# Window attention with a gated branch, one core: the first unit's keys loaded and scored ahead of the feed-forward branch

## The chip, the cores and the metric

The kernel runs on one core of a Trainium2 chip. The metric is device time in microseconds (us); the time before is the median of three runs. Five engines work side by side, each through its own list of instructions in order: TensorE (PE, with its weight loads shown apart as PEld), VectorE (DVE), ScalarE (ACT), GpSimd (POOL) and SyncE (SP), which here does little but issue the large loads. The loads themselves are carried out by 16 DMA engines.

## The reference, cut to what matters

One decode step for two batch rows. A normalized row goes through attention over the last 4096 positions of a key and value cache (32 query heads over 8 key heads of 128), and through a small gated feed-forward branch whose result multiplies the attention's output:

```python
xn = _layernorm(x)                                   # x: (2, 1, 512)
q = (xn @ wq), 32 heads of 128
k, v = k_cache[:, :, -4096:, :], v_cache[:, :, -4096:, :]
s = softmax(q k^T / sqrt(128)) v @ wo                # wq 512 x 4096, wo 4096 x 512
z = gelu(xn @ w_in); z1, z2 = halves of z            # w_in 512 x 1792
y = (z1 * (w_sp * layernorm(z2) + b_sp)) @ w_out     # w_out 896 x 512
out = x + s * silu(y)
```

All is float32. The inputs are read once: w_q and w_o are 8192 KB each, w_in 3584 KB, w_out 1792 KB, and the keys and values in use 65536 KB together.

## The kernel before, in words

**Units.** The 2 batch rows times 8 key heads are taken in pairs: 8 units, numbered by `u.n`, each with one load of keys (`u.k`) and one of values (`u.v`), 4096 KB apiece.

**The ring.** Everything large goes through one tile, `ring`, of four slots of 4096 KB. `enqueue` puts a load into a list and gives it the next slot (w_q takes two); `advance(slot)` marks a slot as free and issues from the head of the list whatever now has its slot. All these loads are issued by SP, in the order of the list, so one that waits for its slot holds back those behind it. The order before is w_q (slots 0 and 1), w_in (2), w_out (3), keys 0 (0), keys 1 (1), values 0 (2), keys 2 (3), values 1 (0), keys 3 (1) and so on, and at the end w_o in pieces. A one-column copy of `rs`, the normalization's factor, into slot 2 stands ahead of the second load, so that this load is issued after it.

**The order on the engines.** PE, DVE, ACT and SP run what is written, in the order in which it is written (the class `InOrder`). First come the queries: `q_ps` on PE, `qT`, `qm` on DVE, `rp` on PE, `qbd` on DVE. Then the feed-forward branch: `z` on PE from w_in; a row of short steps on DVE, ACT and PE (`zs`, `zt`, `zT`, `u`, `mean`, `var`, `hT`); `y` on PE from w_out; `ys`, `yq` and `gate`. Then the units.

**A unit.** Its keys are transposed on DVE in four quarters (`turn`, tile `kt`, three buffers); each quarter is multiplied with the queries on PE (`shares`, tile `sh`), copied by ACT to `shs`, and added into `s` (`add_shares`). The maximum and the exponentials of a unit (`share_max`, tiles `m`, `mg`, `mo`, `nb`; `probs`) come in the next unit, between its first and its second quarter, and its values (`values`, tile `acc`) behind that. Keys are freed after the fourth quarter's transpose, values after `acc`.

**The end.** After the last unit, w_o is multiplied in blocks as its pieces land (`part`, `so`), and `res` is formed with `gate` and written out. `gate` is read nowhere else.

Of the kernel before, what the change touches and what calls it, by code (L numbers as in the profile page):

```python
# [9 lines left out]
F32 = mybir.dt.float32  # L10
AF = mybir.ActivationFunctionType
ALU = mybir.AluOpType
AX = mybir.AxisListType

P = 128
HQ, DH = 32, 128
G = 4
EPS = 1e-5
# [3 lines left out]
def ap(t, offset, dims):  # L22

    return bass.AP(tensor=t.tensor, offset=t.offset + offset, ap=[list(t.ap[0])] + [list(d) for d in dims])
# [18 lines left out]
def kernel(  # L43
# [14 lines left out]
    pe, dve, act, sp = (InOrder(tc, e) for e in (nc.tensor, nc.vector, nc.scalar, nc.sync))  # L58
    B, _, D = x.shape
# [4 lines left out]
    FH = F // 2  # L64
    KT = D // P
    FT = FH // P
    DC = D // G
    SCALE = DH ** -0.5
    NU = B * HKV // 2
# [7 lines left out]
    sb = ctx.enter_context(tc.tile_pool(name="sb", bufs=2))  # L77
# [7 lines left out]
    def enqueue(load, count=1):  # L85

        at = turns[0] % 4
        turns[0] += count
        queue.append((load, range(at, at + count)))
        advance()  # L90

    def advance(*slots):
        for n in slots:
            free[n] = True
        while queue and all(free[n] for n in queue[0][1]):
            load, at = queue.pop(0)
            for n in at:
                free[n] = False
            load(ring[:, at[0] * SLOT : (at[-1] + 1) * SLOT], at[0])

    def const(name, *shape):
        return cst.tile([P, *shape], F32, tag=name, name=name)

    def bank(name, tag):
        return ps.tile([P, 512], F32, tag=tag, name=name, bufs=BANKS[tag])


    weight = {}

    def load_rows(name, w, k):  # L110
        def load(t, at):
            n = k * w.shape[1]
            sp.dma_start(t[:, :n], w.rearrange("(p k) f -> p (k f)", p=P))
            weight[name] = t[:, :n].rearrange("p (k f) -> p k f", k=k)

        return load
# [8 lines left out]
    def load_unit(cache, u, name):  # L125

        first = cache[u.b, 2 * u.w, SK - W :, :]
        src = bass.AP(tensor=first.tensor, offset=first.offset, ap=[[SLOT, P // 2], [SK * DH, 2], [1, SLOT]])

        def load(t, at):  # L130
            sp.dma_start(t, src)
            setattr(u, name, t.rearrange("p (j d) -> p j d", d=DH))
            u.slot[name] = at

        return load
# [4 lines left out]
    units = []  # L140
    for n in range(NU):
        u = Unit()
# [30 lines left out]
    wb1 = cst.tile([1, 2], F32, tag="wb1", name="wb1")  # L173
    act.dma_start(wb1[:, 0:1], bass.AP(tensor=w_sp.tensor, offset=w_sp.offset, ap=[[1, 1], [1, 1]]))
    act.dma_start(wb1[:, 1:2], bass.AP(tensor=b_sp.tensor, offset=b_sp.offset, ap=[[1, 1], [1, 1]]))
    xnT = const("xnT", KT, 32)
    nc.gpsimd.memset(xnT, 0.0)
    ones = const("ones", P)
    nc.gpsimd.memset(ones, 1.0)
    hT = const("hT", FT, 32)  # L180
# [14 lines left out]
    rowm = const("rowm", 32)  # L195
# [4 lines left out]
    def rsqrt(dst, a, tag):  # L200
        t = cst.tile(list(a.shape), F32, tag="rt" + tag, name="rt" + tag)
        act.activation(t, a, AF.Ln)
        act.activation(dst, t, AF.Exp, scale=-0.5)
        dve.tensor_mul(t, dst, dst)
        dve.tensor_mul(t, t, a)
        dve.tensor_scalar(t, t, -0.5, 1.5, op0=ALU.mult, op1=ALU.add)
        dve.tensor_mul(dst, dst, t)
# [9 lines left out]
    rsqrt(rs, va, "x")  # L217

    dve.tensor_copy(ring[:B, 2 * SLOT : 2 * SLOT + 1], rs)
    enqueue(load_rows("in", w_in, KT))  # L220
    enqueue(load_rows("out", w_out, FT))
    win, wout = weight["in"], weight["out"]
    for n in range(NU + 1):
        if n < NU:
            enqueue(load_unit(k_cache, units[n], "k"))
        if n > 0:
            enqueue(load_unit(v_cache, units[n - 1], "v"))
# [41 lines left out]
    for k in range(KT):  # L269
        for r in range(2):  # L270
            for g in range(G):
                c = (r * G + g) * 512
                pe.matmul(
                    pq[r][32 * g : 32 * g + 32, :], xnT[:, k, :], wqt[:, k, c : c + 512],
                    start=(k == 0), stop=(k == KT - 1),
# [17 lines left out]

    def q_of(u, dq):
        return ap(qbd, (u.n * 4 + dq) * 32, [[1, 32]])


    FQ = FH // G
    pz = bank("z", "sh")[:, : 2 * FQ]
    for k in range(KT):  # L300
        for g in range(G):
            pe.matmul(
                pz[32 * g : 32 * g + 32, :], xnT[:, k, :], ap(win[:, k, :], g * FQ, [[FH, 2], [1, FQ]]),
                start=(k == 0), stop=(k == KT - 1),
            )
    advance(2)
    wb_ps = bank("wb_ps", "mo")[:, :2]
    pe.matmul(wb_ps, ones[0:1, :], wb1, start=True, stop=True)
    wb = const("wb", 2)
    dve.tensor_copy(wb, wb_ps)  # L310
    zs = const("zs", 2 * FQ)
    act.activation(zs, pz, AF.Copy)
    zt = const("zt", 2 * FT, 32)
    dve.transpose(zt.rearrange("p j c -> p (j c)"), ap(zs, 0, [[FQ, 2], [1, FT], [FT, 32]]))
    zT = const("zT", 2, FT, B)
    zTf = zT.rearrange("p h j b -> p (h j) b")
    dve.tensor_copy(zTf, zt[:, :, :B])
    uu = const("u", 2, FT, B)
    dve.tensor_mul(uu, zT, zT)
    dve.tensor_scalar(uu, uu, 0.044715, 1.0, op0=ALU.mult, op1=ALU.add)  # L320
    dve.tensor_mul(uu, uu, zT)
    dve.tensor_scalar(uu, uu, -2.0 * math.sqrt(2.0 / math.pi), 80.0, op0=ALU.mult, op1=ALU.min)
    act.activation(uu, uu, AF.Exp)
    dve.tensor_scalar_add(uu, uu, 1.0)
    dve.reciprocal(uu, uu)
    dve.tensor_mul(zT, zT, uu)

    z1, z2, w2 = zT[:, 0], zT[:, 1], uu[:, 0]
    mean, var = const("mean", B), const("var", B)

    def mean_over_rows(dst, src, name):
        pm = bank(name, "mo")[:, : FT * B]
        pe.matmul(pm, ones, src.rearrange("p j b -> p (j b)"), start=True, stop=True)
        dve.reduce_sum(dst, pm.rearrange("p (j b) -> p b j", b=B), axis=AX.X)

    per_b = [[0, FT], [1, B]]
    mean_over_rows(mean, z2, "mean_ps")
    dve.scalar_tensor_tensor(z2, ap(mean, 0, per_b), -1.0 / FH, z2, op0=ALU.mult, op1=ALU.add)
    dve.tensor_mul(w2, z2, z2)
    mean_over_rows(var, w2, "var_ps")  # L340
    dve.tensor_scalar(var, var, 1.0 / FH, EPS, op0=ALU.mult, op1=ALU.add)
    rsqrt(mean, var, "z")
    dve.tensor_mul(z2, z2, ap(mean, 0, per_b))
    dve.tensor_scalar(z2, z2, wb[:, 0:1], wb[:, 1:2], op0=ALU.mult, op1=ALU.add)
    dve.tensor_mul(hT[:, :, 0 : 16 * B : 16], z1, z2)


    def spread_quarters(dst, shares, start=True, stop=True):
        for g in range(G):
            pe.matmul(  # L350
                dst[32 * g : 32 * g + 32, :], rowm, shares[:, g * DC : (g + 1) * DC], start=start, stop=stop,
            )

    yp = bank("y", "sh")
    for j in range(FT):
        g = j % G
        pe.matmul(yp[32 * g : 32 * g + 32, :], hT[:, j, :], wout[:, j, :], start=(j < G), stop=(j >= FT - G))
    advance(3)
    ys = sb.tile([P, D], F32, tag="shs", name="ys")
    act.activation(ys, yp, AF.Copy)  # L360
    y = bank("yq", "mo")[:, :DC]
    spread_quarters(y, ys)
    gate = const("gate", DC)
    dve.tensor_scalar(gate, y, -1.0, 80.0, op0=ALU.mult, op1=ALU.min)
    act.activation(gate, gate, AF.Exp)
    dve.tensor_scalar_add(gate, gate, 1.0)
    dve.reciprocal(gate, gate)
    dve.tensor_mul(gate, gate, y)


    def turn(u, m):

        u.kt[m] = sb.tile([P, JC, DH], F32, tag="kt", name=f"kt{u.n}_{m}", bufs=3)
        dve.transpose(
            u.kt[m].rearrange("p j d -> p (j d)"), u.k[:, JC * m : JC * m + JC, :].rearrange("p j d -> p (j d)")
        )
# [104 lines left out]
    def collect_last(u):  # L481
# [6 lines left out]
        dve.reduce_sum(ol[r, :], t.rearrange("p (j n) -> p n j", j=NCH), axis=AX.X)  # L488
        divide(u.b, ol[r, :], r)

    prev = old = None
    last = units[-1]
    for u in units:
        turn(u, 0)
        shares(u, 0)
        if old is not None and old.n == NU // B - 1:
            divide(0, gather(0))
        if prev is not None:
            share_max(prev)
            probs(prev)  # L500
        turn(u, 1)
        shares(u, 1)
        add_shares(u, 0)
        if prev is not None:
            probs_t(prev)
            weigh(prev)
            if u is not last:
                values(prev)
        for m in range(2, NCH):
            turn(u, m)  # L510
            shares(u, m)
            add_shares(u, m - 1)
        if u is not last and prev is not None:
            scale_out(prev)
        advance(u.slot["k"])
        add_shares(u, NCH - 1)
        if u is not last and prev is not None:
            advance(prev.slot["v"])
            collect(prev)
        old, prev = prev, u  # L520
# [20 lines left out]
    for n in range(EARLY):  # L541
        t, a = blocks[n]
        g = n % G
# [4 lines left out]
    for n in range(EARLY, 32):  # L548
# [3 lines left out]
        for g in range(G):  # L552
            pe.matmul(
                so[32 * g : 32 * g + 32, :], oT[:, n, :], t[:, a, g * DC : (g + 1) * DC],
                start=(n == EARLY), stop=(n == 31),
# [33 lines left out]
```

## Time and profile before

| | |
|---|---|
| median of three runs | 217.49 us (217.29 to 217.51) |
| span of the profiled execution, first to last instruction | 215.6 us; its own time is not listed, the median is 1.9 us above the span |
| read from memory | 89.40 MB, 415 GB/s over the span |
| share of the span that the loads' queue kept the 16 DMA engines | 96.9% |
| busy: PE, DVE, ACT | 144.9, 107.1, 43.7 us |
| mean granted TensorE clock | 0.885 |

Busy times are sums over a whole span, and the engines overlap; none of them is the time by itself. Nearly all instructions stand under one source line, the helper that records the order, so rows are told apart by tile names: in `kt<-ring` the tile left of the arrow is written and that on the right is read. In the timeline a row gives the start, the duration (of a run of like instructions together where it ends in x5), and in brackets the idle time ahead of it and what ended it.

### The profile page before, as it was taken

To read this page: it belongs to the slowest core of one execution; us is meant where nothing else is said; L and a number is where in the kernel's file an instruction comes from. 1 tells how busy PE (TensorE), PEld (TensorE's weight loads), DVE (VectorE), ACT (ScalarE), POOL (GpSimd) and SP (SyncE) were. 2 spreads that over 40 slices of the span, in tenths; PEclk is the share of its full clock that TensorE was granted. 3 is DMA by queue.
4 is the path that set the end of the run, shared out by engine and by line. 5 is a ranking of instruction groups with operands and counts; after the bars stand their busy time and mean duration, and the time that the engine had idled before them with its cause. 6 is when DMAs were issued, how large, how long until landed. Compare 5 with 4: busy or idle time off the path is not lost.

```text
span 215.6 us, 2181 instructions
## 1 busy us (share of the span) xinstructions
PE 144.9 (67%) x848; PEld 40.3 (19%) x848; DVE 107.1 (50%) x161; ACT 43.7 (20%) x108; POOL 4.2 (2%) x22
## 2 busy tenths in 40 slices
PE   0010787224595897699599499459949967987663
PEld 0010222100021222122122132112202211222311
DVE  1140025633995943953936663793585089233101
ACT  2030000331124115114303304130331231241001
POOL 6010000000000000000000000000000000000000
PEclk9999999658599699699799789859975996999998
DMA  9898999999999999999999999999999999999990
GB/s 389 390 389 389 431 423 459 435 438 421 450 395 474 395 453 419 444 432 425 439 404 450 419 444 429 432 432 419 444 413 447 425 432 444 425 435 404 410 376 33
DMA packets 3788, 89.52 MB, mean 415 GB/s; under 512 B 434, under 2 KB 450, under 8 KB 964
## 3 DMA queue, kind: packets, MB, share of 16 engines
q1 hardware_dynamic: 3772, 89.40, 96.9%
q8 instruction: 6, 0.10, 0.2%
q14 instruction: 2, 0.02, 0.0%
q10 hardware_dynamic: 8, 0.00, 0.0%
HBM read 89.40 MB, written 0.00 MB: 415 GB/s over the span
## 4 chain that ended last, share of the span: by engine, by line
DMA 41%; PE 39%; DVE 16%; ACT 2%; issue 2%; DVEq 0%
DMA ring<-in_A_wo_dram 20%; PE sh L37 11%; DMA ring<-in_A_k_cache_dram 11%; DVE kt L37 10%; DMA ring<-in_A_wq_dram 10%; PE s L37 10%; PE acc L37 7%; PE q_ps L37 4%; PE y L37 2%; PE z L37 1%; PE col L37 1%; PE mo L37 1%; DVE gate L37 1%; DVE u L37 1%; DVE qm L37 1%
## 5 line engine op out<-in xcount | busy, mean ns | idle before, releaser
L37 DVE STREAM_TRANSPOSE kt<-ring 128x2048 f32<-128x2048 f32 x32 | 72.2, 2286 | 24.9 <-DMA ring<-in_A_k_cache_dram 24.9
L37 PE MATMUL sh<-kt,qbd 128*32 128x512 f32 x256 | 43.6, 725 | 27.0 <-DVE kt L37 27.0
L37 ACT ACTIVATE shs<-sh 128x512 f32<-128x512 f32 x32 | 19.1, 597 | 99.4 <-PE sh L37 99.4
L37 PE MATMUL s<-shs,add_dq 128*128 128x512 f32 x64 | 39.0, 716 | 0.0
L37 PE MATMUL acc<-ring,pT 128*32 128x512 f32 x256 | 31.3, 614 | 0.0
L37 PEld LDWEIGHTS s<-shs,add_dq 128*128 128x128 f32 x64 | 11.0, 215 | 30.9 <-issue 26.5
L37 PEld LDWEIGHTS sh<-kt,qbd 128*32 128x32 f32 x256 | 7.0, 117 | 46.3 <-issue 38.3
L37 PE MATMUL q_ps<-ring,xnT 128*32 128x512 f32 x64 | 8.8, 713 | 7.6 <-DMA ring<-in_A_wq_dram 7.6
L37 PEld LDWEIGHTS acc<-ring,pT 128*32 128x32 f32 x256 | 7.8, 112 | 22.3 <-issue 17.6
L37 DVE TENSOR_REDUCE m<-s 128x2 f32<-128x512 f32 x8 | 5.4, 680 | 13.0 <-PE s L37 12.9
L37 PE MATMUL xnT_ps<-ident,xn 2*128 2x2 f32 x4 | 0.6, 252 | 14.5 <-DVE xn L37 14.5
L37 ACT ACTIVATE o<-acc,diag 128x128 f32<-128x128 f32 x30 | 8.6, 374 | 4.9 <-PE acc L37 4.9
L37 PE MATMUL part<-ring,oT 128*32 128x512 f32 x56 | 6.6, 597 | 3.5 <-DMA ring<-in_A_wo_dram 3.5
L37 ACT ACTIVATE p<-s,nb 128x256 f32<-128x256 f32 x16 | 7.6, 488 | 6.6 <-DVE nb L37 6.4
L37 DVE STREAM_TRANSPOSE qT<-q_ps 128x512 f32<-128x512 f32 x2 | 1.4, 717 | 14.4 <-PE q_ps L37 14.3
L37 PE MATMUL col<-o,sel 128*32 128x512 f32 x14 | 7.3, 601 | 0.0
L37 DVE TENSOR_TENSOR res<-so,gate 128x128 f32<-128x128 f32 x1 | 0.3, 292 | 11.5 <-PE so L37 11.5
L37 DVE STREAM_TRANSPOSE pT<-p 128x512 f32<-128x512 f32 x8 | 5.4, 674 | 1.2 <-ACT p L37 1.2
L37 PE MATMUL y<-ring,hT 128*32 128x512 f32 x14 | 3.3, 996 | 3.8 <-DVE hT L37 3.8
L37 ACT ACTIVATE zs<-z 128x448 f32<-128x448 f32 x1 | 0.5, 544 | 24.7 <-PE z L37 24.7
L37 ACT ACT_TABLE_LOAD x4 | 5.1, 1283 | 0.8 <-PEq L575 0.7
L37 PEld LDWEIGHTS q_ps<-ring,xnT 128*32 128x32 f32 x64 | 2.5, 130 | 13.1 <-issue 13.1
(114 smaller groups left out, 62.2 us busy)
## 6 DMA issues: line engine op xcount, KB each, us to landing
ring<-in_A_k_cache_dram SPq DMA_DIRECT2D x8, 4096.0 KB, 20.0
ring<-in_A_v_cache_dram SPq DMA_DIRECT2D x8, 4096.0 KB, 28.1
ring<-in_A_wo_dram SPq DMA_DIRECT2D x1, 4096.0 KB, 33.2
ring<-in_B_w_in_dram SPq DMA_DIRECT2D x1, 3584.0 KB, 17.1
ring<-in_A_wo_dram SPq DMA_DIRECT2D x1, 2048.0 KB
ring<-in_B_w_out_dram SPq DMA_DIRECT2D x1, 1792.0 KB, 21.0
ring<-in_A_wo_dram SPq DMA_DIRECT2D x1, 1024.0 KB
ring<-in_A_wo_dram SPq DMA_DIRECT2D x4, 256.0 KB, 17.6
```

What stands on the lines that cost most here:

```text
L37: return self.tc.keep_in_program_order(call(*args, **kwargs))
```

## The change

Keys 0 are put into the list right behind w_q, and w_in and w_out behind them. The loop leaves keys 0 out. The branch becomes the function `form_gate`, called ahead of unit 1, so that all of unit 0's transposes, products and sums stand ahead of `z` on the engines. Keys 0 now have slot 2, w_in slot 3, w_out slot 0; from keys 1 on each load has the slot that it had. `advance` is called with 3 after `z` (before: 2) and with 0 after `y` (before: 3).

```diff
     dve.tensor_copy(ring[:B, 2 * SLOT : 2 * SLOT + 1], rs)
+    enqueue(load_unit(k_cache, units[0], "k"))
     enqueue(load_rows("in", w_in, KT))
     enqueue(load_rows("out", w_out, FT))
-    win, wout = weight["in"], weight["out"]
     for n in range(NU + 1):
-        if n < NU:
+        if 0 < n < NU:
             enqueue(load_unit(k_cache, units[n], "k"))
         if n > 0:
             enqueue(load_unit(v_cache, units[n - 1], "v"))
...
-    FQ = FH // G
-    pz = bank("z", "sh")[:, : 2 * FQ]
-    for k in range(KT):
...
-    advance(2)
...
-        pe.matmul(yp[32 * g : 32 * g + 32, :], hT[:, j, :], wout[:, j, :], start=(j < G), stop=(j >= FT - G))
-    advance(3)
...
+    def form_gate():
+        FQ = FH // G
+        pz = bank("z", "sh")[:, : 2 * FQ]
+        for k in range(KT):
...
+        advance(3)
...
+            pe.matmul(yp[32 * g : 32 * g + 32, :], hT[:, j, :], weight["out"][:, j, :], start=(j < G), stop=(j >= FT - G))
+        advance(0)
...
+        dve.tensor_mul(gate, gate, y)
+        return gate
+
     prev = old = None
     last = units[-1]
     for u in units:
+        if u.n == 1:
+            gate = form_gate()
         turn(u, 0)
         shares(u, 0)
```

SP's list of loads before, from its start (`in_A_wq_dram` is w_q, `in_B_w_in_dram` w_in, `in_B_w_out_dram` w_out, and the caches are keys and values by name):

```order
L37 DMA ring<-in_A_wq_dram 128x16384
L37 DMA ring<-in_B_w_in_dram 128x7168
L37 DMA ring<-in_B_w_out_dram 128x3584
L37 DMA ring<-in_A_k_cache_dram 128x1x8192 x2
L37 DMA ring<-in_A_v_cache_dram 128x1x8192
```

And after:

```order
L37 DMA ring<-in_A_wq_dram 128x16384
L37 DMA ring<-in_A_k_cache_dram 128x1x8192
L37 DMA ring<-in_B_w_in_dram 128x7168
L37 DMA ring<-in_B_w_out_dram 128x3584
L37 DMA ring<-in_A_k_cache_dram 128x1x8192
L37 DMA ring<-in_A_v_cache_dram 128x1x8192
```

Keys 0 moved ahead of both weights; the list is the same from keys 1 on.

On PE, behind the queries' `rp`, stood before the branch and then unit 0 (the last row is unit 0's first product):

```order
L37 MATMUL rp<-qm,same 128x256
L37 MATMUL z<-ring,xnT 32x448 x16
L37 MATMUL wb_ps<-wb_74,ones 128x2
L37 MATMUL mean_ps<-zT,ones 128x14
L37 MATMUL var_ps<-u,ones 128x14
L37 MATMUL y<-ring,hT 32x512 x7
L37 MATMUL yq<-ys,rowm 32x128 x4
L37 MATMUL sh_0_283<-kt_0_281,qbd 32x512 x4
```

And after, from the same place:

```order
L37 MATMUL rp<-qm,same 128x256
L37 MATMUL sh_0_203<-kt_0_201,qbd 32x512 x4
L37 MATMUL sh_1_212<-kt_1_210,qbd 32x512 x4
L37 MATMUL s_219<-shs_0_208,add_dq 128x512
L37 MATMUL sh_2_223<-kt_2_221,qbd 32x512 x4
L37 MATMUL s_219<-shs_1_217,add_dq 128x512
L37 MATMUL sh_3_233<-kt_3_231,qbd 32x512 x4
L37 MATMUL s_219<-shs_2_228,add_dq 128x512
L37 MATMUL s_219<-shs_3_238,add_dq 128x512
L37 MATMUL z<-ring,xnT 32x448 x16
```

`z` and all behind it in the branch now wait for the eight groups of unit 0; unit 1's first product, which stood behind unit 0's last sum, stands behind `yq`.

On DVE the last rows of the branch and the transposes of units 0 and 1 stood before as follows:

```order
L37 TENSOR_TENSOR gate<-gate,yq 128x128
L37 STREAM_TRANSPOSE kt_0_281<-ring 128x2048
L37 STREAM_TRANSPOSE kt_1_290<-ring 128x2048
L37 STREAM_TRANSPOSE kt_2_301<-ring 128x2048
L37 STREAM_TRANSPOSE kt_3_311<-ring 128x2048
L37 STREAM_TRANSPOSE kt_0_323<-ring 128x2048
```

And after, from the queries' last step to the branch's first two:

```order
L37 TENSOR_SCALAR qbd<-rp,grpm 128x64x4 x4
L37 STREAM_TRANSPOSE kt_0_201<-ring 128x2048
L37 STREAM_TRANSPOSE kt_1_210<-ring 128x2048
L37 STREAM_TRANSPOSE kt_2_221<-ring 128x2048
L37 STREAM_TRANSPOSE kt_3_231<-ring 128x2048
L37 COPY wb<-wb_ps 128x2
L37 STREAM_TRANSPOSE zt<-zs 128x448
```

Unit 0's four transposes moved from behind `gate` to ahead of `wb`; unit 1's first one (`kt_0_323`) now follows `gate` directly.

More of the change, by code (lines that the diff above doesn't have):

```diff
@@ L295, in q_of @@
         return ap(qbd, (u.n * 4 + dq) * 32, [[1, 32]])
-    FQ = FH // G
-    pz = bank("z", "sh")[:, : 2 * FQ]
-    for k in range(KT):
[L301 to L305, printed above, removed]
-    advance(2)
-    wb_ps = bank("wb_ps", "mo")[:, :2]
-    pe.matmul(wb_ps, ones[0:1, :], wb1, start=True, stop=True)
-    wb = const("wb", 2)
@@ L310 @@
[L310 to L345, printed above, removed]
@@ L348, in spread_quarters @@
[L348 to L356, printed above, removed]
-        pe.matmul(yp[32 * g : 32 * g + 32, :], hT[:, j, :], wout[:, j, :], start=(j < G), stop=(j >= FT - G))
-    advance(3)
-    ys = sb.tile([P, D], F32, tag="shs", name="ys")
-    act.activation(ys, yp, AF.Copy)
@@ L361 @@
[L361 to L368, printed above, removed]
     def turn(u, m):
@@ L489, in collect_last, with spread_quarters, mean_over_rows @@
         divide(u.b, ol[r, :], r)
+    def spread_quarters(dst, shares, start=True, stop=True):
+        for g in range(G):
+            pe.matmul(
+                dst[32 * g : 32 * g + 32, :], rowm, shares[:, g * DC : (g + 1) * DC], start=start, stop=stop,
+            )
+    def form_gate():
+        FQ = FH // G
+        pz = bank("z", "sh")[:, : 2 * FQ]
+        for k in range(KT):
+            for g in range(G):
+                pe.matmul(
+                    pz[32 * g : 32 * g + 32, :], xnT[:, k, :], ap(weight["in"][:, k, :], g * FQ, [[FH, 2], [1, FQ]]),
+                    start=(k == 0), stop=(k == KT - 1),
+                )
+        advance(3)
+        wb_ps = bank("wb_ps", "mo")[:, :2]
+        pe.matmul(wb_ps, ones[0:1, :], wb1, start=True, stop=True)
+        wb = const("wb", 2)
+        dve.tensor_copy(wb, wb_ps)
+        zs = const("zs", 2 * FQ)
+        act.activation(zs, pz, AF.Copy)
+        zt = const("zt", 2 * FT, 32)
+        dve.transpose(zt.rearrange("p j c -> p (j c)"), ap(zs, 0, [[FQ, 2], [1, FT], [FT, 32]]))
+        zT = const("zT", 2, FT, B)
+        zTf = zT.rearrange("p h j b -> p (h j) b")
+        dve.tensor_copy(zTf, zt[:, :, :B])
+        uu = const("u", 2, FT, B)
+        dve.tensor_mul(uu, zT, zT)
+        dve.tensor_scalar(uu, uu, 0.044715, 1.0, op0=ALU.mult, op1=ALU.add)
+        dve.tensor_mul(uu, uu, zT)
+        dve.tensor_scalar(uu, uu, -2.0 * math.sqrt(2.0 / math.pi), 80.0, op0=ALU.mult, op1=ALU.min)
+        act.activation(uu, uu, AF.Exp)
+        dve.tensor_scalar_add(uu, uu, 1.0)
+        dve.reciprocal(uu, uu)
+        dve.tensor_mul(zT, zT, uu)
+        z1, z2, w2 = zT[:, 0], zT[:, 1], uu[:, 0]
+        mean, var = const("mean", B), const("var", B)
+        def mean_over_rows(dst, src, name):
+            pm = bank(name, "mo")[:, : FT * B]
+            pe.matmul(pm, ones, src.rearrange("p j b -> p (j b)"), start=True, stop=True)
+            dve.reduce_sum(dst, pm.rearrange("p (j b) -> p b j", b=B), axis=AX.X)
+        per_b = [[0, FT], [1, B]]
+        mean_over_rows(mean, z2, "mean_ps")
+        dve.scalar_tensor_tensor(z2, ap(mean, 0, per_b), -1.0 / FH, z2, op0=ALU.mult, op1=ALU.add)
+        dve.tensor_mul(w2, z2, z2)
+        mean_over_rows(var, w2, "var_ps")
+        dve.tensor_scalar(var, var, 1.0 / FH, EPS, op0=ALU.mult, op1=ALU.add)
+        rsqrt(mean, var, "z")
+        dve.tensor_mul(z2, z2, ap(mean, 0, per_b))
+        dve.tensor_scalar(z2, z2, wb[:, 0:1], wb[:, 1:2], op0=ALU.mult, op1=ALU.add)
+        dve.tensor_mul(hT[:, :, 0 : 16 * B : 16], z1, z2)
+        yp = bank("y", "sh")
+        for j in range(FT):
+            g = j % G
+            pe.matmul(yp[32 * g : 32 * g + 32, :], hT[:, j, :], weight["out"][:, j, :], start=(j < G), stop=(j >= FT - G))
+        advance(0)
+        ys = sb.tile([P, D], F32, tag="shs", name="ys")
+        act.activation(ys, yp, AF.Copy)
+        y = bank("yq", "mo")[:, :DC]
+        spread_quarters(y, ys)
+        gate = const("gate", DC)
+        dve.tensor_scalar(gate, y, -1.0, 80.0, op0=ALU.mult, op1=ALU.min)
+        act.activation(gate, gate, AF.Exp)
+        dve.tensor_scalar_add(gate, gate, 1.0)
+        dve.reciprocal(gate, gate)
+        dve.tensor_mul(gate, gate, y)
+        return gate
```

## The prediction
> **What bounds the kernel now.** I read the page's slices first, then the windows, then the loads' issues. In the slices the second row is the busy share of the 16 DMA engines in tenths:
>
> ```profile
> DMA  9898999999999999999999999999999999999990
> GB/s 389 390 389 389 431 423 459 435 438 421 450 395 474 395 453 419 444 432 425 439 404 450 419 444 429 432 432 419 444 413 447 425 432 444 425 435 404 410 376 33
> q1 hardware_dynamic: 3772, 89.40, 96.9%
> ```
>
> The engines of the loads are busy in every slice but the last, while PE and DVE have idle slices. Two windows show how steady that is (the last two columns are the DMA share and GB/s):
>
> ```profile
> 25.00:195.00 170.00, 129.36 (x712) 34.71 (x706) 100.11 (x131) 39.34 (x100) 0.00 (x0) 0.86 1.00 431
> 2.00:212.00 210.00, 144.44 (x842) 40.19 (x843) 105.94 (x158) 42.47 (x108) 2.75 (x12) 0.89 0.99 423
> ```
>
> From 25 to 195 us the share is 1.00 at 431 GB/s. So the stream of loads is the bound: 89.4 MB at the whole stream's 423 GB/s are 211 us. What is left is a start of about a microsecond and the tail. The chain of waits seems to say something else, since over its first 130 us it runs through PE and DVE; but it ends in loads that were in a queue:
>
> ```profile
> 125.88 4.41 DVE kt L37 x2
> 130.31 22.99 DMA ring<-in_A_k_cache_dram
> 168.72 33.24 DMA ring<-in_A_wo_dram
> 211.99 0.47 PE so L37 x8
> ```
>
> A load of 4096 KB that "takes" 22.99 us at 431 GB/s (4.19 MB, 9.7 us of work) stood over 13 us behind others. The instruction that released its issue was therefore not what it waited for, and what the chain shows ahead of 130.31 is not a bound. The second sign is DVE, which from unit 3 on waits for keys; the bracket is the idle time ahead of the row:
>
> ```profile
> 95.10 2.31 DVE L37 STREAM_TRANSPOSE kt<-ring 128x2048 f32<-128x2048 f32 x1 [2.37 <-DMA ring<-in_A_k_cache_dram]
> 114.57 2.31 DVE L37 STREAM_TRANSPOSE kt<-ring 128x2048 f32<-128x2048 f32 x1 [4.89 <-DMA ring<-in_A_k_cache_dram]
> DVE kt L37 <- DMA ring<-in_A_k_cache_dram: 24.9, 5, 8.0
> ```
>
> Five units of the eight wait for their keys, 24.9 us together. Keys 3 landed at 95.10 and keys 4 at 114.57, with one load of values between: 19.47 us for two loads, 9.74 us each.
>
> **The change part by part.** *Loads.* No byte, no load and no shape is added; two small weights and one load of keys change places. If the stream never runs dry its end stays, so the term is 0. It remains to show that it doesn't run dry. SP's issues, and the first two weights' time from issue to landing (last number):
>
> ```profile
> 13.92 0.34 SPq L37 DMA_DIRECT2D ring<-in_B_w_in_dram  x1
> 28.10 3.99 SPq L37 DMA_DIRECT2D ring<-in_A_k_cache_dram  x2
> 50.60 0.54 SPq L37 DMA_DIRECT2D ring<-in_A_k_cache_dram  x1
> 62.78 0.54 SPq L37 DMA_DIRECT2D ring<-in_A_v_cache_dram  x1
> 75.84 0.54 SPq L37 DMA_DIRECT2D ring<-in_A_k_cache_dram  x1
> 92.76 0.54 SPq L37 DMA_DIRECT2D ring<-in_A_k_cache_dram  x1
> ring<-in_B_w_in_dram SPq DMA_DIRECT2D x1, 3584.0 KB, 17.1
> ring<-in_B_w_out_dram SPq DMA_DIRECT2D x1, 1792.0 KB, 21.0
> ```
>
> w_in landed at 13.92 + 17.1 = 31.0, w_out (issued right behind it) at 35.3. w_q landed when PE began the queries:
>
> ```profile
> 22.67 8.81 PE L37 MATMUL q_ps<-ring,xnT 128*32 128x512 f32 x64 [7.57 <-DMA ring<-in_A_wq_dram]
> 34.40 3.21 PE L37 MATMUL z<-ring,xnT 128*32 128x448 f32 x32
> ```
>
> So w_in takes 8.4 us and w_out 4.3. Landings in the new order: w_q 22.7, keys 0 32.4, w_in 40.8, w_out 45.1, and then as before keys 1 54.8, values 0 64.6, keys 2 74.3, values 1 84.1, keys 3 at about 94 (95.10 in the trace, so these deadlines are on the early, strict side).
>
> *Unit 0.* Its rows before, and the branch's last:
>
> ```profile
> 34.50 1.66 DVE L37 TENSOR_SCALAR qbd<-rp,grpm 128x256 f32<-128x256 f32 x4 [0.85 <-PE rp L37]
> 53.87 11.07 DVE L37 STREAM_TRANSPOSE kt<-ring 128x2048 f32<-128x2048 f32 x5
> 66.50 0.69 DVE L37 TENSOR_REDUCE m<-s 128x2 f32<-128x512 f32 x1 [1.56 <-PE s L37]
> 68.53 2.31 DVE L37 STREAM_TRANSPOSE kt<-ring 128x2048 f32<-128x2048 f32 x1
> ```
>
> Keys 0 are there at 32.4, the queries (`qbd`) are formed at 36.2, so the first transpose moves from 53.87 to 36.2. The four take 4 x 2.21 = 8.9 us (11.07 over 5) and end at 45.1. Unit 0's sums ended at 66.50, 12.6 us after the first transpose: now at 48.8.
>
> *The branch.* `z` stands on PE behind those sums: it starts at 48.8, though w_in is there at 40.8; before it started at 34.40. From `z` to the end of `gate` DVE came to 53.87, 19.5 us; that chain is serial and is taken whole: it ends at 68.3. Nobody but the last multiplication at 212 us reads `gate`, which covers its lateness. But unit 1's first transpose stands right behind it on DVE. Before it started at 53.87 + 4 x 2.21 = 62.7; now at 68.3. Of those 5.6 us the 1.56 us come back that `m` waited for the sums, which are now long done: 68.3 + 2.2 + (68.53 - 66.50) = 72.5 for unit 1's second quarter against 68.53. **Unit 1 comes 4.0 us later**, not earlier: unit 0's tail on PE lay beside unit 1's first transpose before, and now nothing lies beside the branch's short steps.
>
> *The queue, issue by issue* (each must come before the landing of the load ahead). w_out now waits for slot 0, which the first half of the queries frees at 28.10, against w_in's 40.8: 12.7 us to spare; keys 1, behind it, follow at some 31.5 as before (the second issue of the row that starts at 28.10 and lasts 3.99, less half a microsecond). Values 0 wait for unit 0's fourth transpose: 45.1 against 54.8. Keys 2 wait for `z`: 52.0 against 64.6. Values 1 wait for `y`: before, that was 50.60 - 34.40 = 16.2 us behind `z`, now 65.0 against 74.3. Keys 3 wait for unit 1's fourth transpose: 75.84 + 4.0 = 79.8 against 84.1. Keys 4: 92.76 + 4.0 = 96.8 against 104.8 (their own landing less 9.74). The narrowest is keys 3 with 4.3 us (8.3 before). From issue to first byte I allow 1.3 us, an estimate from the first slice of 5.4 us, which moved as many bytes as the three behind it though the first load was issued only at 0.73 us; 3.0 us remain. Later issues meet more slack, because units 3 and 4 wait for keys: 2.37 and then 4.89 us of idle take up 4.0, and from unit 4 on everything stands where it stood.
>
> [...] PE's clock matters to this margin; the same matmul of 512 columns took (min, median, max):
>
> ```profile
> L37 PE MATMUL y<-ring,hT x14: 754/1060/1061, 47.2 to 49.8; 128*32 128x512 f32 x14
> L37 PE MATMUL part<-ring,oT x56: 590/592/617, 202.1 to 209.9; 128*32 128x512 f32 x56
> 47.20:50.60 3.40, 3.33 (x14) 0.58 (x14) 0.00 (x0) 0.00 (x0) 0.00 (x0) 0.57 0.98 424
> 40.00:45.00 5.00, 1.19 (x4) 1.00 (x4) 1.83 (x10) 2.66 (x4) 0.00 (x0) 0.50 0.98 419
> 58.50:66.50 8.00, 7.99 (x36) 1.83 (x40) 6.44 (x3) 2.12 (x4) 0.00 (x0) 0.88 1.06 455
> ```
>
> `y` ran at a granted clock of 0.57 behind a stretch in which PE had little to do (0.50). `z` ran right behind the queries; now it comes behind unit 0's products, whose clock was 0.88. I take 3.2 us for it. At the low clock it would be 3.2 x 1060 / 592 = 5.7 us, and keys 3 would be issued at 82.3: still before 84.1, with half a microsecond left after the first byte's 1.3. [...]
>
> *The tail* is untouched:
>
> ```profile
> 211.50 0.92 PE L37 MATMUL so<-ring,oT 128*32 128x128 f32 x16
> 212.81 0.29 DVE L37 TENSOR_TENSOR res<-res,x 128x128 f32<-128x128 f32 x1
> ```
>
> *Sum:* loads 0, unit 0 and branch 0 (beside the loads), queue 0, tail 0. The span stays 215.6 us, and with the 1.9 us by which the median of the runs lies above it, 217.5.
>
> **The rivals.** *Slower: unit 1's lateness drains the queue at keys 3.* For it: the narrowest place becomes half as wide, and the branch's length in its new place is borrowed from another one. Against it: it takes 3.0 us more than the 4.0 worked out. Bounds: with `z` and unit 0's sums at full clock the lateness is some 3 us, with `z` slow 6.5. If the sums and unit 1's products were slow too (another 2 to 4 us), it would be up to 10, and the stream would stand still for up to 3.5 us, which nothing gives back, since the stream is full afterwards. It decides from an issue of keys 3 at 82.8 on; half of that price gives 217.5 + 1.7 = 219.2. Chance 0.10. *Faster: the stream itself runs better.* The first slices show 389 GB/s against 431 later. If the large load of keys behind w_q let all of it go at 431, the 211 us of stream would shrink by 1 - 423/431, 1.9 per cent or 4 us: 213.5. Against it: w_q, the same load as before, fills those four slices. Chance 0.03. [...] *Faster: the chain of waits is right after all,* and work done 17.7 us earlier shortens it. By the same chain, though, unit 1 is 4.0 us late, so it would rather give 217.5 + 4.0 = 221.5; DVE's waits for keys speak against both signs, and I leave 0.03 to the gain (at most to the floor of the stream, some 215) and 0.02 to the loss. *The change doesn't do what it says:* if keys 0's landing gave nothing to unit 0, all would stand as before, at 217.5; that lies within the forecast.
>
> **How the numbers follow.** No change has 0.82, slower 0.12 (queue 0.10, chain 0.02), faster 0.06. What a measurement can tell from no change is about 0.2 per cent, 0.43 us; the three runs spread over 0.22. The time is the likeliest case's, 217.5; its own range is 217.1 to 217.9. The range is 217.0 to 218.3: it leaves out the gains and the upper part of the loss, together less than 0.15, and takes in a stand-still of up to 0.8 us.
>
> **What the changed profile would show.** Right: the DMA row full of nines with no dip between 70 and 90 us; unit 0's first transpose near 36, `z` near 49, `gate` done near 68, keys 3 issued near 80; DVE's wait for keys 3 gone, that for keys 4 near 3.3 us instead of 4.89, and keys 4 and later at the same times as before. Wrong: keys 3 issued after 83 and less than 400 GB/s in the windows from 80 to 90; keys 4 landing other than at 114.6 by more than half a microsecond; or an end that moves while DVE's waits for keys stay.

## The result, and the profile after

The changed kernel takes 219.72 us (median of five runs, 219.15 to 219.90) against 217.29 us, the median of five runs of the kernel before. The medians are 2.43 us apart; the ratio on record, which is not the quotient of these two medians, is 1.0088 (95% interval 1.0070 to 1.0106). The change makes the kernel slower by about 1 per cent. The profiled execution took 219.9 us and has a span of 218.0, 2.4 more than before. Here and below, ratios leave out slow executions, more than 1.5 per cent above the fastest of the same kernel, while medians and ranges take in all.

The slices of the page after (DMA share in tenths, GB/s, and the queue's total):

```profile
DMA  9889999999999997989899999999999999999980
GB/s 385 386 385 403 463 420 437 400 439 466 403 463 398 463 403 289 460 385 481 385 481 383 469 397 463 403 463 403 460 403 457 406 451 415 451 415 422 411 347 17
q1 hardware_dynamic: 3772, 89.40, 96.1%
```

The sixteenth slice (81.8 to 87.2 us) has 289 GB/s where its neighbours have 403 and 460; before, no slice but the last two was below 389. SP's issues around it, from the timeline, and the window from 80 us (last two columns: DMA share, GB/s):

```profile
66.82 0.53 SPq L37 DMA_DIRECT2D ring<-in_A_v_cache_dram  x1
82.86 0.54 SPq L37 DMA_DIRECT2D ring<-in_A_k_cache_dram  x1
80.00:85.00 5.00, 5.00 (x34) 1.29 (x38) 5.00 (x3) 0.56 (x1) 0.00 (x0) 0.80 0.86 321
85.00:90.00 5.00, 5.00 (x30) 1.21 (x22) 0.02 (x1) 2.06 (x6) 0.00 (x0) 1.00 0.98 410
```

Keys 3 are issued at 82.86 instead of 75.84. The two windows lack some 1.6 us of loads against 433 GB/s ((433 - 321) x 5 / 433 = 1.3 and 0.3). What delayed the issue is seen on DVE and PE:

```profile
37.25 8.88 DVE L37 STREAM_TRANSPOSE kt<-ring 128x2048 f32<-128x2048 f32 x4
50.11 3.21 PE L37 MATMUL z<-ring,xnT 128*32 128x448 f32 x32
70.32 2.30 DVE L37 STREAM_TRANSPOSE kt<-ring 128x2048 f32<-128x2048 f32 x1
75.54 2.31 DVE L37 STREAM_TRANSPOSE kt<-ring 128x2048 f32<-128x2048 f32 x1
107.44 0.69 DVE L37 TENSOR_REDUCE m<-s 128x2 f32<-128x512 f32 x1 [5.12 <-PE s L37]
DVE kt L37 <- DMA ring<-in_A_k_cache_dram: 6.2, 2, 3.9
```

Unit 0 starts 16.6 us earlier (37.25 against 53.87), and unit 1's second transpose comes 7.0 us later (75.54 against 68.53). DVE waits for keys in two units instead of five, 6.2 us instead of 24.9: the engines now run behind the loads through most of the kernel. The end, where w_o is multiplied:

```profile
205.13 7.77 PE L37 MATMUL part<-ring,oT 128*32 128x512 f32 x56 [0.68 <-DVE oT L37]
213.93 0.80 PE L37 MATMUL so<-ring,oT 128*32 128x128 f32 x16
205.00:210.00 5.00, 4.87 (x32) 1.27 (x36) 0.07 (x1) 0.00 (x0) 0.00 (x0) 0.67 0.96 397
```

and the same stretch before:

```profile
202.09 3.64 PE L37 MATMUL part<-ring,oT 128*32 128x512 f32 x32 [1.74 <-DMA ring<-in_A_wo_dram]
206.91 1.92 PE L37 MATMUL part<-ring,oT 128*32 128x512 f32 x16 [1.17 <-DMA ring<-in_A_wo_dram]
209.41 1.07 PE L37 MATMUL part<-ring,oT 128*32 128x512 f32 x8 [0.58 <-DMA ring<-in_A_wo_dram]
```

Before, PE waited for w_o three times, 3.5 us together. After, it waits for no load there: the 56 products run in one go, with a granted clock of 0.67 in the window from 205 us. The loads end late as well, as the windows from 210 us show, before and then after (the last number is GB/s):

```profile
210.00:215.00 5.00, 2.19 (x48) 0.95 (x40) 0.58 (x2) 0.60 (x1) 0.00 (x0) 0.89 0.12 47
210.00:215.00 5.00, 4.49 (x68) 1.54 (x60) 0.20 (x1) 0.60 (x1) 0.00 (x0) 1.00 0.42 157
```

At 210 us 0.24 MB were still to come before and 0.79 MB after, about 1.3 us of loads more. So there are two candidates for the 2.4 us: the stream, which stood still, and the engines, which come late to the end.

### The profile page after: what moved, and what is told of

It is laid out like the page before. It is cut to its first block, busy times and chain, and to the rows that moved or that the text cites. A ratio compares the mean times of both kernels' runs of the same rounds, so it can differ in the third digit from the quotient of the medians.

```text
span 218.0 us, 2176 instructions
## 1 busy us (share of the span) xinstructions
PE 148.0 (68%) x848; PEld 40.9 (19%) x848; DVE 106.9 (49%) x161; ACT 43.7 (20%) x108; POOL 4.2 (2%) x22
## 4 chain that ended last, share of the span: by engine, by line
PE 65%; DVE 19%; DMA 10%; ACT 3%; issue 2%; DVEq 0%; ACTq 0%
PE s L37 18%; PE sh L37 16%; PE acc L37 13%; DVE kt L37 10%; DMA ring<-in_A_wq_dram 10%; PE q_ps L37 4%; PE part L37 4%; PE col L37 2%; PE y L37 2%; PE mo L37 2%; PE z L37 1%; DVE qbd L37 1%; DVE gate L37 1%; DVE u L37 1%; DVE mx L37 1%
## 5 line engine op out<-in xcount | busy, mean ns | idle before, releaser
L37 PE MATMUL sh<-kt,qbd 128*32 128x512 f32 x256 | 45.1, 710 | 28.3 <-DVE kt L37 28.3
L37 PE MATMUL s<-shs,add_dq 128*128 128x512 f32 x64 | 40.9, 745 | 0.0
L37 PEld LDWEIGHTS s<-shs,add_dq 128*128 128x128 f32 x64 | 11.3, 219 | 29.3 <-issue 24.9
L37 PE MATMUL q_ps<-ring,xnT 128*32 128x512 f32 x64 | 9.3, 749 | 7.5 <-DMA ring<-in_A_wq_dram 7.5
L37 PE MATMUL part<-ring,oT 128*32 128x512 f32 x56 | 7.8, 715 | 0.7 <-DVE oT L37 0.7
L37 DVE TENSOR_REDUCE mx<-mo 128x1 f32<-128x16 f32 x8 | 1.4, 174 | 8.3 <-PE mo L37 8.3
## 6 DMA issues: line engine op xcount, KB each, us to landing
ring<-in_B_w_out_dram SPq DMA_DIRECT2D x1, 1792.0 KB, 18.7
```

The lines of the kernel that those rows point to most:

```text
L37: return self.tc.keep_in_program_order(call(*args, **kwargs))
```

## The experiments

**Lateness alone.** The kernel before, with transposes ahead of unit 1 whose result is not used:

```diff
     for u in units:
+        if u.n == 1:
+            for _ in range(3):
+                dve.transpose(spare, u.k[:, :JC, :].rearrange("p j d -> p (j d)"))
         turn(u, 0)
```

> The kernel before with three further transposes on DVE (3 x 2.21 = 6.6 us, their result is not used) ahead of unit 1; loads and branch as before. Queue theory (unit 1's lateness drains the queue of loads at keys 3): keys 3 issued at 75.84 + 6.6 = 82.4, a stand-still of about 1 us near 83 us, 218.4 to 219.6. Rival order of loads (keys 0 between w_q and the weights makes the stream itself slower): the order is that of before, so 217.3. Rival engines' chain (the lateness is carried along PE and DVE to the end, not through the loads): 219 to 220 as well, but the keys of units 6 and 7 land as before.

Measured: 220.9 us, ratio 1.0153 (1.0111 to 1.0196), runs from 219.81 to 224.4. With the loads in their old order the time rises all the same, so the order of the loads is not needed for the loss. It rises by more than either theory said. The trace doesn't tell them apart: the profiled execution was the longest of the six (224.4 us), in it unit 0 itself came 3.1 us late (56.99) and unit 1 9.4 us, keys 3 were issued at 85.29, and DVE waited for unit 7's keys until 177.20 instead of 172.86.

With two transposes instead of three:

> The kernel before with two further transposes (4.4 us) ahead of unit 1, loads and branch as before. By the step on record (4 us of lateness cost nothing): 217.3 to 217.7. Theory of two ends: no stand-still where PE's clock holds up (keys 3 issued at 80.3), the chain 4.4 us late at unit 1 and some 1 to 2 at the end, 217.5 to 218.8, with a wide spread from the clock. Order of loads as a cause: 217.4.

Measured: 217.89 us, 1.0029 (1.0004 to 1.0054), eight of twelve runs at 218.1 or below and the others up to 221.2. In the profiled execution unit 1 was 3.6 us late, keys 3 were issued at 79.47, and the span was 215.6, as before. The median lies above the 217.7 that the step on record allows, and within what the theory of two ends expected. Some 4 us of lateness are free in most executions, not in all.

**Keys 3 in two halves**, the first issued ahead of unit 1's third transpose: the stand-still is taken away and unit 1 left late. `load_half` issues one half; its definition, and the second half in the list's place of keys 3, are left out here.

```diff
+        if u.n == 1:
+            units[3].slot["k"] = u.slot["k"]
+            load_half(units[3], 0)
         for m in range(2, NCH):
             turn(u, m)
```

> The changed kernel with the load of keys 3 cut in two: the first half is issued behind unit 1's second transpose (near 77.9 us), the second behind its fourth (82.9). Unit 1 stays as late as in the changed kernel. Queue theory: no stand-still, 217.2 to 217.7. Rival engines' chain: still 219.0 to 219.9, since nothing on PE, DVE or ACT comes earlier. Rival order of loads: 219.0 to 219.9.

Measured: 219.24 us, 1.0081 (1.0049 to 1.0112). The queue theory said 217.2 to 217.7 and falls as the only cause. Its window and its end:

```profile
80.00:85.00 5.00, 5.00 (x38) 1.16 (x40) 4.46 (x3) 0.00 (x1) 0.00 (x0) 0.84 0.92 393
74.99 2.30 DVE L37 STREAM_TRANSPOSE kt<-ring 128x2048 f32<-128x2048 f32 x1
204.67 7.78 PE L37 MATMUL part<-ring,oT 128*32 128x512 f32 x56 [0.68 <-DVE oT L37]
213.48 0.62 PE L37 MATMUL so<-ring,oT 128*32 128x128 f32 x16
210.00:215.00 5.00, 3.75 (x64) 1.53 (x56) 0.58 (x2) 0.60 (x1) 0.00 (x0) 1.00 0.16 60
```

The loads hardly stop any more (393 GB/s instead of 321), and at 210 us 0.30 MB were left, nearly as little as before. Unit 1 is 6.5 us late, and PE still runs the last 56 products in one go, without a wait for w_o. Here the engines' chain alone sets the end.

**Two ends.** So the time is the later of two: the last landing of w_o with what follows it, and the engines' chain with its 56 products. The next three kernels put two short matmuls ahead of these products, so that PE has less idle time there.

```diff
     t = gather(last.b)
+    w2 = bank("warm_end", "sh")
+    pe.matmul(w2, ones, qT[:, :512], start=True, stop=True)
...
     collect_last(last)
+    pe.matmul(w2[:, :256], ones, qT[:, :256], start=True, stop=True)
```

With keys 3 in halves:

> The kernel with keys 3 in two halves (no stand-still of the stream, unit 1 as late as in the changed kernel) plus two further matmuls on PE, 512 columns behind the last oT product and 256 behind ol, so that PE has less idle time ahead of the last w_o products; their result is not used. Theory of two ends (the time is set by the later of the stream's last landing and the engines' chain, whose last stretch ran at half clock for 3.4 us): the 56 part matmuls take 6.6 instead of 7.8 us, 217.8 to 218.4, against 219.24 without the two matmuls. Queue theory alone (the engines' chain doesn't set the end): 219.2, no change. If the stream's last landing sets it in that kernel: 219.2, no change.

Measured: 218.40 us, 1.0032 (1.0012 to 1.0053). In the changed kernel, with its stand-still:

> The changed kernel with the two further matmuls ahead of the last w_o products and nothing else. Theory of two ends: its stream lands 1.7 to 2.3 us late by the stand-still, so the faster part matmuls gain little, 218.9 to 219.6 (against 218.4 where the stand-still was away as well). If only the engines' chain sets the end: about 218.6, as much gained as with keys 3 in halves.

Measured: 218.93 us, 1.0054 (1.0034 to 1.0074). In the kernel before, as a control:

> Control: the kernel before with the same two matmuls ahead of the last w_o products. The stream's last landing sets the end there, so both theories say 217.3 to 217.7; a gain of more than half a microsecond would mean that PE's last stretch sets the end before, too.

Measured: 217.54 us, 0.9991 (0.9973 to 1.0009). The rows of the first two, in this order (the execution of the second is the longest of its eight, 219.83 us):

```profile
205.51 6.21 PE L37 MATMUL part<-ring,oT 128*32 128x512 f32 x56
```

```profile
206.13 5.36 PE L37 MATMUL part<-ring,oT 128*32 128x512 f32 x48
211.88 1.07 PE L37 MATMUL part<-ring,oT 128*32 128x512 f32 x8 [0.39 <-DMA ring<-in_A_wo_dram]
```

With keys 3 in halves the 56 products take 6.2 instead of 7.8 us, at a granted clock of 1.00 instead of 0.71 in the window from 205 us, and the time falls by 0.8 us. With the stand-still left in, PE waits for w_o again (0.39): the stream's end has taken over in that trace. The kernel before gains nothing. Away with the stand-still or with the slow products alone, most of the loss stays. The times by themselves don't separate the two ends, though: the two matmuls gained 0.8 us with the stand-still left in, too (219.72 to 218.93). That there are two ends rests on the waits for w_o in the traces.

**PE's clock in the branch.** Four groups of three further matmuls in PE's idle stretches between 34 and 70 us (three of the calls are left out here):

```diff
+    def keep_busy(n):
+        w = bank("warm", "acc")
+        for i in range(n):
+            pe.matmul(w, ones, qT[:, :512], start=True, stop=True)
...
         dve.tensor_copy(wb, wb_ps)
+        keep_busy(3)
```

> The changed kernel with four groups of three further matmuls of 512 columns on PE (their result is not used), in its idle stretches: ahead of unit 0, behind the wb, var and yq products. If the half clock of PE in the branch's stretch is what made unit 1 3 us later than the 4.0 worked out: y 3.6 to 2.0 us, unit 1's first product 1.9 to 1.1, keys 3 issued at 80.5 to 81.5 and a time of 217.3 to 218.3. If the clock has no part in it: keys 3 at 82.9, 219.0 to 219.9, or later where the further matmuls stand in the way.

Measured: 217.57 us, 1.0005 (0.9987 to 1.0024); ten of twelve runs lie between 217.40 and 217.93, two at 218.81 and 219.09. The loss is gone in the median though order and loads are those of the changed kernel. The profiled execution is the one at 218.81. In it `y` took half as long as in the changed kernel (3.63 us), but the 56 products at the end still took 7.9 us and waited for no load:

```profile
63.80 1.92 PE L37 MATMUL y<-ring,hT 128*32 128x512 f32 x14 [1.58 <-DVE hT L37]
204.26 7.89 PE L37 MATMUL part<-ring,oT 128*32 128x512 f32 x56 [0.68 <-DVE oT L37]
```

With the two matmuls at the end as well:

> The kernel whose PE is kept busy through the branch (217.57) plus the same two matmuls ahead of the last w_o products. Theory of two ends: unit 1 is 4.7 us late, the chain ends within a microsecond of the stream, and the runs near 219 (part at half clock) go away: median 217.4 to 217.7, highest below 218.3. If the spread has another cause: runs near 219 remain.

Measured: 217.52 us, 0.9993 (0.9981 to 1.0006), highest 217.83. The window from 58 to 82 us of the changed kernel and then of this one, with this one's second transpose of unit 1 and its issue of keys 3:

```profile
58.00:82.00 24.00, 11.44 (x48) 2.88 (x52) 13.43 (x24) 4.81 (x11) 0.00 (x0) 0.50 1.00 430
58.00:82.00 24.00, 18.73 (x90) 5.08 (x93) 16.22 (x24) 4.82 (x11) 0.00 (x0) 0.79 1.00 430
71.63 2.31 DVE L37 STREAM_TRANSPOSE kt<-ring 128x2048 f32<-128x2048 f32 x1
78.94 0.53 SPq L37 DMA_DIRECT2D ring<-in_A_k_cache_dram  x1
```

In the changed kernel PE ran at half clock for all of those 24 us (0.50, the number ahead of the last two). With PE kept busy, unit 1's second transpose comes at 71.63, 3.1 us late, and keys 3 are issued at 78.94.

**Unit 1 earlier, without further work.** Its first transpose is put behind `hT`, into DVE's wait for `y`, and its first product behind `yq`; the loop then leaves both out for unit 1 (not shown):

```diff
         dve.tensor_mul(hT[:, :, 0 : 16 * B : 16], z1, z2)
+        turn(units[1], 0)
...
         spread_quarters(y, ys)
+        shares(units[1], 0)
         gate = const("gate", DC)
```

> The changed kernel with unit 1's first transpose put on DVE behind hT (in the wait for y) and its first product on PE behind yq. Queue theory: unit 1's second transpose comes some 3 us earlier, keys 3 are issued near 79.7, no stand-still, 217.2 to 217.8. Rival engines' chain: 3 of 7 us of lateness taken away, about 218.3. Rival order of loads: 219.0 to 219.9.

Measured: 220.25 us, 1.0092 (1.0057 to 1.0127), with two runs at 218.3 and 218.7. This missed, by a fault of the edit:

```profile
70.25 0.60 ACT L37 ACTIVATE shs<-sh 128x512 f32<-128x512 f32 x1 [2.48 <-PE sh L37]
70.74 0.30 ACT L37 ACTIVATE gate<-gate 128x128 f32<-128x128 f32 x1
```

The product's copy stands on ACT ahead of the gate's exponential and holds it up by the 2 us that were gained. With `shares(units[1], 0)` moved behind that exponential:

> The changed kernel with unit 1's first transpose behind hT, its first product on PE behind yq, and (unlike the earlier trial) that product's copy on ACT behind the gate's exponential, which it had held up by 2 us. No further matmuls: PE's clock is left as it is. Theory of two ends: gate done near 70.2, unit 1's second transpose near 72.4 (4 us late instead of 7), keys 3 issued near 79.7, no stand-still, 217.4 to 218.2. If the half clock itself is what costs, by whatever way: 219 to 220.

Measured: 217.49 us, 1.0000 (0.9985 to 1.0015).

```profile
72.81 2.30 DVE L37 STREAM_TRANSPOSE kt<-ring 128x2048 f32<-128x2048 f32 x1
80.12 0.54 SPq L37 DMA_DIRECT2D ring<-in_A_k_cache_dram  x1
58.00:82.00 24.00, 13.99 (x72) 3.82 (x76) 16.39 (x26) 4.82 (x11) 0.00 (x0) 0.57 1.00 429
202.30 3.64 PE L37 MATMUL part<-ring,oT 128*32 128x512 f32 x32 [0.68 <-DVE oT L37]
206.93 1.92 PE L37 MATMUL part<-ring,oT 128*32 128x512 f32 x16 [0.99 <-DMA ring<-in_A_wo_dram]
```

This one separates clock and lateness: PE is still near half clock (0.57) in the branch, but unit 1 is 4.3 us late instead of 7.0, and the whole loss is gone. The low clock in the branch costs only through the lateness here (217.49 us at 0.57). This version of the changed order needs no further work and is as fast as before, not faster, since PE waits for w_o at the end again (0.99): the stream sets the end of both.

**The halves of the change.**

> Half of the change: unit 0's scores ahead of the branch, the loads in the order of before (w_in, w_out, keys 0). Keys 0 land at 45.4, so z starts near 59, and values 0 wait for z's slot: issued near 62 while the stream has run out at 54.8. Theory of two ends: a stand-still of some 8 us there and about 2 more at keys 2 or 3, 226 to 229. If late engines cost nothing because the units wait for keys anyway: 217.5.

> The other half: loads in the order of the changed kernel (keys 0, w_in, w_out), the branch ahead of unit 0 as before. Keys 0 hold slot 2 until unit 0's transposes, which stand behind the branch: values 0 issued near 70, the stream empty from 54.8. Theory of two ends: a stand-still of some 15 to 16 us, 232 to 235. If an earlier load of keys 0 is worth something by itself: below 217.5.

Measured, in two runs each: 230.10 us, 1.0569 (1.0526 to 1.0612), and 237.00 us, 1.0887 (1.0845 to 1.0928). Both lose more than expected. The slots are the reason, as these rows show for the engines' order alone and then for the loads alone:

```profile
62.20 0.53 SPq L37 DMA_DIRECT2D ring<-in_A_v_cache_dram  x1
55.00:60.00 5.00, 5.00 (x30) 1.43 (x30) 0.00 (x0) 1.19 (x2) 0.00 (x0) 1.00 0.01 3
70.00:75.00 5.00, 3.26 (x14) 0.58 (x14) 1.30 (x7) 0.08 (x1) 0.00 (x0) 0.53 0.73 315
```

```profile
72.27 0.53 SPq L37 DMA_DIRECT2D ring<-in_A_v_cache_dram  x1
60.00:65.00 5.00, 0.46 (x11) 0.16 (x8) 3.32 (x5) 0.91 (x2) 0.00 (x0) 0.84 0.00 0
65.00:70.00 5.00, 3.93 (x17) 0.57 (x17) 5.00 (x4) 0.60 (x1) 0.00 (x0) 0.50 0.00 0
```

Each half makes values 0 wait for a slot while the stream has run out. Here a stand-still goes to the end in full: in the loads alone the windows from 50 to 75 us have DMA shares of 0.74, 0.01, 0.00, 0.00 and 0.34, 5 x 3.91 = 19.6 us lost, and the time is 19.5 us above before.

## Why the prediction was wrong, point by point

The sum put four terms at nothing. Two of them, the queue and the tail, were not nothing, and both for the same reason: unit 1 came later than worked out, and its lateness was not taken up on the way.

**The bound.** Right: the stream bounds the kernel before (a DMA share of 1.00 at 431 GB/s from 25 to 195 us), and in the loads alone a stand-still of 19.6 us was paid with 19.5.

**Unit 0 and z.** Nearly right: the first transpose at 37.25 (36.2 worked out), `z` at 50.11 (48.8) and 3.21 us long at a granted clock of 1.00. About 1.0 us of the shift lies in the queries, which the change leaves alone: they took 9.3 instead of 8.8 us on PE, and `rp` 1.2 instead of 0.7. They ended at 32.13 us instead of 31.48; in three experiments they ended at 31.83 and 31.37 with the loads in the new order (PE kept busy, the loads alone) and at 31.89 in the old one (the engines' order alone), and `rp` took 0.67 in all three. So this 1.0 is taken for a difference between two executions.

**Unit 1's lateness, 4.0 us: mis-sized; it is 7.0.** The 3.0 us are the 1.0 just named, 0.3 in unit 0's sums, 0.7 in the branch (from `z` 20.2 us instead of 19.5; `y` and `yq` at half clock are 0.5 of it), and 1.0 between unit 1's first and second transpose: its first product ran at half clock (1.9 instead of 1.1 us), and `mo`, which DVE waits for, stands behind it. The product before, then `y` and the product after:

```profile
66.39 1.06 PE L37 MATMUL sh<-kt,qbd 128*32 128x512 f32 x8
63.13 3.63 PE L37 MATMUL y<-ring,hT 128*32 128x512 f32 x14 [4.25 <-DVE hT L37]
72.68 1.93 PE L37 MATMUL sh<-kt,qbd 128*32 128x512 f32 x8 [4.55 <-DVE kt L37]
```

The prediction asked what the clock would do to `z`, which it left alone; it fell on the products behind `z`. The trace has the clock at 0.50 from 58 to 82 us, with idle stretches of 4.25 and 4.55 us and PE busy for 11.4 of the 24; with the further matmuls, here and at the end, it is 0.79 over the same 24 us, with PE busy for 18.7. How long a stretch of idleness or of work it takes to move the clock, no run shows.

**The queue, put at 0.** The lateness held against the margin was too small, and the margin of 3.0 us was too wide. Its deadline, 84.1, is a landing as a waiting engine sees it; by the bytes moved the stream runs out earlier. The loads up to values 1 are 34048 KB (34.9 MB), and in both kernels the first 80 us moved 33.8 MB (422 GB/s); at the 416 GB/s that the kernel before has from 80 to 85 us, the rest takes until some 82.6. The 1.3 us to the first byte don't follow from the slice that the prediction names, but are about right: with the stream empty, values 0 of the two halves of the change were issued at 62.20 and 72.27, and at 105 GB/s in the windows from 60 and from 70 us 0.53 MB had come by 65 and 75 us, 1.2 us' worth at 431 GB/s; so the first bytes came some 1.5 us after the issue, an estimate. So keys 3 had to be issued by about 81.3, an estimate, 1.5 us behind the 79.8 worked out; even the prediction's 82.3 for a slow `z` would have been too late. The runs agree: with keys 3 issued at 80.12 and 80.58 the window from 80 to 85 us has 416 and 413 GB/s (416 before), at 82.86 it has 321; with the issue at 82.08 (the first trial of unit 1 early) DVE waits for unit 6's keys until 155.03 instead of 153.43. The rival "unit 1's lateness drains the queue at keys 3" (chance 0.10, from an issue at 82.8, 219.2 us) is what half of the result looks like. The other half is the loss under "the chain of waits is right after all" (0.02): the late units reached the end.

**"2.37 and then 4.89 us of idle take up 4.0": wrong, and with a smaller lateness as well.** DVE's waits for keys in units 3 and 4 were not slack. In unit 3 before, DVE waited 2.37 us for keys and then, at `m`, 2.54 for PE's sums; after, it waits 5.12 for PE's sums alone, and `m` comes at 107.44 instead of 99.95, still 7.5 us late. The row before is

```profile
99.95 0.69 DVE L37 TENSOR_REDUCE m<-s 128x2 f32<-128x512 f32 x1 [2.54 <-PE s L37]
```

PE was the one that set the pace there. A smaller lateness passes through as well: in the version with unit 1 4.3 us late, unit 4's second transpose is 4.8 us late (124.22 against 119.40). The true slack lies in units 5 to 7 and at the waits for w_o: when the last `oT` is formed the lateness is down to 4.1 us (the w_o products start at 205.13; before, they could have started at some 201.0 but for their wait), against 3.5 us of waits for w_o.

**The tail: "untouched" was wrong.** Once the engines' chain came late, its last 56 products were the end, and they ran at half clock for part of the time (0.50 in each microsecond from 205 to 208 us, 1.00 from 209): 7.8 us against 6.2 with the two matmuls and keys 3 in halves.

**The sum.** The forecast, 217.5, holds for the change with unit 1 only 3.1 to 4.3 us late, as the two versions at 217.52 and 217.49 show. In the changed kernel as it is, the engines' chain is the end that the trace shows (+2.4 by the last `so`, 213.93 against 211.50, without a wait for w_o). The stream's end is close behind: +1.3 by the bytes left at 210 us, +2.4 by the keys of unit 7, which DVE awaits until 175.29 instead of 172.86.

**Left open.** These two figures for the stream differ. The windows near 83 us lack 1.6 us of loads, and by 175 us the windows of 5 us add up to 0.67 MB less than before, 1.5 us: the stream loses next to nothing more on the way. Unit 7's keys are seen 0.9 us later than the bytes moved account for, and why isn't settled. When the last piece of w_o landed in the changed kernel its trace doesn't show either, since nothing waits for it there.

## What to carry to other kernels

Where loads bound a kernel, the engines' slack is what is left at the end of their own chain, not the sum of one engine's waits for loads (here 3.5 us of waits for w_o against DVE's 24.9 for keys): such a wait may only stand in for a wait on another engine that would come next, as DVE's 2.37 us for keys and 2.54 for PE's sums became 5.12 for the sums. Before moving short serial steps to a place where PE has little else to do, price everything behind them at the low clock that the trace shows in such a place (here 0.50 with PE busy for 11.4 of 24 us, and `y` at 3.63 us instead of 1.92). A move that is free by the sum should be held against its smallest margin twice: at the next issue of the stream, and at the end of the chain.

## What was not expected of the hardware

Two matmuls of 1.1 and 0.7 us, with no result that anyone reads, made the 56 products behind them take 6.2 instead of 7.8 us and the kernel (with keys 3 in halves) 0.8 us shorter, and twelve such matmuls in the branch made the changed kernel some 2 us shorter (217.57 against 219.72): work added to an idle PE paid for itself. And the spread goes with PE's clock, though no run separates it from other causes. In the first trial of unit 1 early, with unit 1 some 6 us late, four runs at a mean granted clock of 0.859 took 220.2 to 220.4 us and two at 0.866 took 218.3 and 218.7; with both stretches kept busy all twelve runs lay between 217.28 and 217.83.
